# Lambda times alpha1 as one spread row, and a later place for the third batch's q loads, in a pooled-attention and residual-MLP kernel

## The chip, the cores and the metric

The kernel runs on one core of a Trainium2 chip, in one launch. The metric is the device time of one execution in microseconds (us), the median of several runs. In the profile PE is the matrix engine (PEld its weight loads), DVE, ACT and POOL are the vector, scalar and general engines, SP is the engine whose queue issues most transfers. PE, DVE, ACT, POOL and SP each work through their own instructions in order and wait for each other by semaphores.

## The reference

Eight batches, eight heads, 576 rows, head width 64. First attention with keys and values averaged over groups of 8 rows; then, on the heads side by side (x: 8 × 576 × 512), a residual block that mixes rows and then channels:

```python
k_p = k.reshape(B, H, Sp, 8, D).mean(axis=3);  v_p = ...          # Sp = 72
attn = softmax(scale * q @ k_p^T);  x = heads_side_by_side(attn @ v_p)
a1  = alpha1 * x + beta1
tok = einsum('ts,bsd->btd', w_tok, a1)
u   = x + lam * tok
a2  = alpha2 * u + beta2
out = u + lam * (maximum(a2 @ w_ch1, 0) @ w_ch2)                  # 512 -> 2048 -> 512
```

lam, alpha1, beta1, alpha2 and beta2 are vectors of 512.

## The kernel before, in words

The order of the work is written out by hand; there is no automatic scheduler. Batch 0's attention stands as a straight list of calls. From then on nine blocks of 512 rows (`n` from 0; four chunks of 128 rows each) go through the MLP, and beside block n the attention of batch n + 1 is placed. For each block a list `todo` of (due time, call) is filled and sorted; the due times only order the calls, and so the instructions of every engine. PSUM has six rotating buffers (`gp`) and two more (`psB`).

Attention of one head: `att_F` transposes q, `att_K` pools and transposes k, `att_S` or `att_S4` makes the scores and their exponentials (ET), `att_AV` multiplies by the pooled v and divides (reciprocal L562, product L564 into `x_tm`). `att_X` (L578) and `rest_X` (L571) multiply x by `lamal_bc`, lambda times alpha1 on all 128 partitions, and give `xs`, the operand of the row mix. `mix_T` (L614) multiplies w_tok by xs and adds x, giving u. ACT casts u to bf16 (L622), and for blocks after the first a transfer on SP's queue transposes it into `u_fm` (L633). `mlp_A` (L662) is the first MLP product; it takes a whole block's u_fm. `mlp_B` (L682) is the second.

The vectors lam, beta1 and alpha1 are loaded as rows into the tile `vecs` (row 0 of it is lam, row 2 alpha1). Before the change `spread_lam` multiplies a column of ones by lam's row in fp32 on PE (L304), which puts lam on all partitions, and ACT copies it to `lam_bc` (L305). `spread_al1` does that with one half of alpha1 (L311), and DVE multiplies it by lam_bc into a half of lamal_bc (L312). The first half is made before the first scores, the second between the scores of heads 6 and 7. lam_bc is also used by `scale_w2` (L721, sixteen pieces of w2 times lambda on DVE) and in block 0's output (L688). `bias_row` (L284) makes beta1 · lam, `more_constants` sets four constant regions that are needed only once w_tok is set up, and `keep_warm(n)` (L605) issues n matmuls on zeros whose result nobody reads.

At the start q, k and v come by transfers that POOL issues. The loads of batch 2 are issued during block 0: remainder rows (`load_rem`, L148), k (`load_k`, L93) and v (`load_v`, L160) from SP's queue, each behind a small DVE memset (the gate, due 15.3 to 15.4) that keeps them from starting earlier, and q (`load_q_bf`, L79) from POOL's queue, due 14.0 and 14.1. POOL does batch 1's att_X in three pieces (heads 2 and 3, 0 and 1, 4 and 5, due 13.8, 15.3 and 17.1), DVE the last (heads 6 and 7, due 18.8).

Of the kernel before, what the change touches and what calls it, by code (L numbers as in the profile page):

```python
# [11 lines left out]
ALU = mybir.AluOpType  # L12
# [11 lines left out]
def kernel(  # L24
# [18 lines left out]
    nc = tc.nc  # L43
# [8 lines left out]
    def gp(name):  # L52
        return psA.tile([P, 512], FP, tag="gp", name=name)
# [146 lines left out]
    lam_bc = const.tile([P, DM], FP, tag="lam_bc", name="lam_bc")  # L200
    lamal_bc = const.tile([P, DM], FP, tag="lamal_bc", name="lamal_bc")
# [3 lines left out]
    vecs = const.tile([65, 3, DM], FP, tag="vecs", name="vecs")  # L205
    ones_row = const.tile([1, P], FP, tag="ones_row", name="ones_row")
# [60 lines left out]
    for i in range(2):  # L267
# [11 lines left out]
                            in1=pool_v[0:32, 1:16:2], op=ALU.add)  # L279
    nc.vector.tensor_reduce(out=pool_rem, in_=pool_each, op=ALU.max, axis=AX.X)  # L280

    def bias_row(i):
        p0 = 64 - 64 * i
        nc.vector.tensor_tensor(out=xs_pool[i][p0:p0 + 1, 4, :], in0=vecs[p0:p0 + 1, 1],  # L284
                                in1=vecs[p0:p0 + 1, 0], op=ALU.mult)
# [5 lines left out]
    def more_constants():  # L291
        nc.vector.memset(ones_bf, 1.0)
        nc.vector.memset(ones_lo[0:64], 1.0)
        nc.vector.memset(ones_lo[64:128], 0.0)
        nc.vector.memset(wtT[:, :, S:640], 0.0)
# [2 lines left out]
        behind.memset(al2_bc[:, 0:1], 0.0)  # L298
        nc.sync.dma_start(out=al2_bc, in_=moe_alpha2.unsqueeze(0).to_broadcast((P, DM)))

    def spread_lam():

        ps = gp("ps_bc")
        nc.tensor.matmul(out=ps, lhsT=ones_row, rhs=vecs[0:1, 0])  # L304
        nc.scalar.copy(out=lam_bc, in_=ps)  # L305

    def spread_al1(half):

        ps = gp("ps_bc")[:, 0:256]
        cols = slice(256 * half, 256 * half + 256)  # L310
        nc.tensor.matmul(out=ps, lhsT=ones_row, rhs=vecs[0:1, 2, cols])  # L311
        nc.vector.tensor_tensor(out=lamal_bc[:, cols], in0=lam_bc[:, cols], in1=ps, op=ALU.mult)  # L312

    def setup_vectors():
        ps = gp("ps_vec")
# [115 lines left out]
    def double_k(u):  # L431

        nc.vector.tensor_copy(out=st1[0]["k"][u][:, :, 4], in_=st1[0]["k"][u][:, :, 0])
        if u == 0:
            cast_rem_k(nc.vector)
# [50 lines left out]
    def att_S(b, h):  # L486
        st = st1[b]
        u, r, hh = h // 4, h // 2 % 2, h % 2
        ET = ET_pool[u][:, h % 4]
        for half in range(2):  # L490
            n0, n = 256 * half, 256 + 64 * half
            ps_sc = gp("ps_sc")
            nc.tensor.matmul(out=ps_sc[0:SPG, 0:256], lhsT=kpT_pool[u][:, half, h % 4, :],  # L493
                             rhs=st["qT"][u][:, 2 * (h % 4):2 * (h % 4) + 2, :])
            if half:
                nc.tensor.matmul(out=ps_sc[0:SPG, 256:320], lhsT=kpT_pool[u][:, hh, h % 4, :],
                                 rhs=st["rem_qT"][:, :, h // 2::4].rearrange("p c i -> p i c"))
            nc.scalar.activation(out=ET[:, n0:n0 + n], in_=ps_sc[0:SPG, 0:n],
                                 func=AF.Exp, bias=0.0, scale=0.125)
        st["ET"][h] = ET  # L500
# [100 lines left out]
    def keep_warm(count):  # L601

        ps = psB.tile([P, DM], FP, tag="ch", bufs=2, name="ps_warm")
        for _ in range(count):
            nc.tensor.matmul(out=ps, lhsT=warm[:, 0:P], rhs=warm)  # L605
# [207 lines left out]
    att_F(0, 0)  # L813
    att_F(0, 1)
    cast_rem(0, nc.vector)
    more_constants()
    keep_warm(1)
    att_Frem(0, nc.scalar.copy)
    keep_warm(1)
    spread_lam()  # L820
    double_k(0)
    att_K(0, 0, None)
    spread_al1(0)
    bias_row(0)
    att_S(0, 0)
    att_S(0, 1)
    first_V(0, 0)
# [17 lines left out]
    att_S(0, 5)  # L845
    att_AV(0, 4)
    att_S(0, 6)
    spread_al1(1)
    att_AV(0, 5)
    att_X(0, 4, 6, nc.gpsimd, False)  # L850
    att_S(0, 7)
# [91 lines left out]
    for n in range(NBLK):  # L943
        todo = []
        for j in range(0 if n else 4, NJ):
            if n == 0 and j < 8:
                todo.append((j, lambda j=j: mlp_A(0, j, 0, 256)))
                todo.append((j + (1.01 if j < 7 else 0.3), lambda j=j: mlp_A(0, j, 256, 512)))
            else:
                at = 8 * (j // 4 % 2) + 4 * (j // 8) + j % 4 if n >= FIRST else j  # L950
                todo.append((at, lambda j=j: mlp_A(n, j)))
        for m in range(4 if n < FIRST else 0):
            for part in range(4):
                at = 16 + 2 * part + (m if m < 2 else 6 + m)
                todo.append((at, lambda m=m, part=part: mlp_B(n, m, part)))
        if n == 0:
            for i in range(3):
                for cc in range(4):
                    todo.append((17.0 + 2.0 * i + 0.5 * cc, lambda i=i, cc=cc: scale_w1(i, cc)))
            for piece, at in enumerate((13.9, 15.3, 19.2, 19.4, 24.5, 24.9, 25.3, 25.7, 26.9, 27.9)):  # L960
                todo.append((at, lambda k=piece: scale_w2(k // 4, k % 4)))
        if n == FIRST - 1:
            for piece, at in enumerate((0.5, 2.6, 5.2, 8.4, 10.9, 13.3)):
                todo.append((at, lambda k=piece + 10: scale_w2(k // 4, k % 4)))
            for s, i in enumerate((1, 3, 2)):
                for g in range(2):
                    todo.append((23.2 + 2.6 * s + 1.3 * g, lambda i=i, g=g: weight_sum(i, g)))
        if n == FIRST:
            for g in range(2):
                todo.append((1.2 + g, lambda g=g: weight_sum(4, g)))  # L970
        if n >= FIRST:
            last = n == NBLK - 1
            when = ((3, (4.6, 14.6)), (1, (8.6, 18.86)), (2, (8.8, 18.98)), (4, (22.3, 23.0)))
            if last:
                when = ((3, (4.6, 12.6)), (1, (8.6, 16.1)), (2, (8.8, 16.2)), (4, (18.6, 19.6)))
            for i, at in when:
                for g in range(2):
                    todo.append((at[g], lambda i=i, g=g: hidden_sum(n, i, g)))
            order = (1, 2, 6, 5, 7, 4, 3) if last else (1, 2, 4, 5, 6, 3, 7)
            for s, i in enumerate(order):  # L980
                for pp in range(2):
                    todo.append((16 + 2 * s + pp, lambda i=i, pp=pp: product(n, i, pp)))
                for part in range(2 if i == 7 else 1):
                    todo.append((17.05 + 2 * s + (1.9 if i == 1 and not last else 0) + 0.01 * part,
                                 lambda i=i, part=part: gather(n, i, part)))
            if last:
                for m in range(2):
                    todo.append((19.1, lambda m=m: store(n, m, 0, HALF)))
                    todo.append((25.2, lambda m=m: store(n, 2 + m, HALF, DM)))
                    todo.append((27.2, lambda m=m: store(  # L990
                        n, 2 + m, 0, HALF, (nc.sync, nc.scalar))))
                    todo.append((29.2, lambda m=m: store(
                        n, m, HALF, DM, ((nc.sync, nc.scalar)[m],) * 2)))
            else:
                for m in range(4):
                    todo.append((27.2 if m < 2 else 29.2, lambda m=m: store(n, m)))
        if n == 0:
            todo.append((6.2, lambda: setup_rowsum(4)))
            todo.append((8.3, setup_wtok_odd))
            for g in range(2, 4):  # L1000
                todo.append((4 * g - 0.8, lambda g=g: setup_bias(range(4 * g, 4 * g + 4))))
        b = n + 1
        if b < B:
            todo += attention(b)
            if b + 1 < B:
                new_batch(b + 1)
                gate = nc.vector if b == 1 else None
                for u in range(2):
                    at = (15.31 if b == 1 else 21.0) + 0.01 * u
                    todo.append((at, lambda b=b, u=u: load_k(b + 1, u, gate)))  # L1010
                    at = {1: 14.0, 2: 6.5}.get(b, 0.4) + 0.1 * u
                    todo.append((at, lambda b=b, u=u: load_q_bf(
                        b + 1, u, nc.vector if b == 2 else None)))
                    at = 15.35 + 0.01 * u if b == 1 else (6.7 if b == 2 else 3.5) + 4.0 * u
                    todo.append((at, lambda b=b, u=u: load_v(
                        b + 1, u, behind=nc.vector if b < 3 else None)))
                todo.append((15.3 if b == 1 else 20.9, lambda b=b: load_rem(b + 1, behind=gate)))
        for _, do in sorted(todo, key=lambda x: x[0]):
            do()
# [30 lines left out]
```

## Time and profile before

| | |
|---|---|
| time, median of 3 runs (lowest, highest) | 334.12 us (333.59, 334.47) |
| the profiled execution's own time, its span | 334.57 us, 332.9 us |
| PE / DVE / ACT / POOL busy, share of the span | 98% / 70% / 53% / 28% |
| costliest groups: L662, L785 (blocks from 2 on), L614 on PE | 133.7, 53.6 + 22.6, 44.9 us busy |
| second half of lamal_bc: L311 on PE, L312 on DVE | begin at 18.56 and 19.29 us |
| first matmul of the row mix, batch 0 and batch 1 | 22.81 and 55.48 us |
| first L662 of block 1 | 69.75 us |
| mean granted PE clock | 0.993 |

The span runs from the first instruction to the last; the time holds 1.67 us more around it. A busy PE in these profiles is not PE at its peak: the ends of matmuls are modelled, and neighbouring matmuls overlap, so where rates matter I go by the distance from one start to the next. In rows of a timeline the columns are start, length (both us), engine, line, operation, output<-input and shape; brackets hold the idle time before, and what ended it. The granted clock is a share of full speed.

### The profile page before, as it was taken

What the parts mean: (1) busy time and instruction counts of PE and PEld (TensorE: products, weight loads), DVE (VectorE), ACT (ScalarE), POOL (GpSimd) and SP (SyncE); (2) the same over time, 40 slices, a digit from 0 to 9 for tenths busy, and PEclk for the clock granted to TensorE, in tenths of its full rate; (3) what the DMA queues carried; (4) which work ended last, traced back from release to release, by engine and by line L of the source; (5) the groups of instructions that cost most, each with busy time, mean ns of one, the idle gap of its engine ahead of it and who ended that gap; (6) DMA issues with size and microseconds to landing.
All of it is one profiled execution on the core that took longest, in us unless ns stands there. A gap on an engine that the chain in (4) does not pass through costs nothing.

```text
span 332.9 us, 6509 instructions
## 1 busy us (share of the span) xinstructions
PE 325.5 (98%) x2531; PEld 209.2 (63%) x2531; DVE 234.5 (70%) x485; ACT 175.6 (53%) x322; POOL 94.8 (28%) x110
## 2 busy tenths in 40 slices
PE   6999999999999999999999999999999999999995
PEld 2667754455544567656775676558765866586584
DVE  6674189999769969677967797877778783263263
ACT  3584989448522871288128812682268325703710
POOL 8667828601237001900271027102510200000000
PEclk9799999999999999999999999999999999999999
DMA  8999979994994983399549943996340045003003
GB/s 117 198 210 270 271 159 206 208 227 87 146 246 105 211 159 121 72 223 181 152 89 219 182 136 73 187 189 194 61 140 2 0 61 145 2 0 127 1 32 97
DMA packets 66472, 45.81 MB, mean 138 GB/s; under 512 B 34397, under 2 KB 57061, under 8 KB 66442
## 3 DMA queue, kind: packets, MB, share of 16 engines
q1 hardware_dynamic: 52092, 32.67, 42.8%
q0 software_dynamic: 13824, 12.40, 22.8%
q8 instruction: 20, 0.33, 0.4%
q10 hardware_dynamic: 526, 0.34, 0.4%
q14 instruction: 10, 0.08, 0.1%
HBM read 38.30 MB, written 9.44 MB: 143 GB/s over the span
## 4 chain that ended last, share of the span: by engine, by line
PE 90%; DMA 5%; DVE 2%; POOL 1%; issue 0%; SPq 0%; ACTq 0%; ACT 0%; DVEq 0%; POOLq 0%
PE ps_h L662 36%; PE ps_w L785 26%; PE ps_tok L614 11%; PE ps_ch L682 7%; DMA rem_raw<-in_k_dram 3%; PE ps_s L513 2%; PE ps_av L556 2%; DMA rem_raw<-in_q_dram 2%; PE ps_kp L445 1%; PE ps_sc L493 1%; PE ps_r L520 1%; DVE x_tm L564 1%; PE ps_av L560 1%; DVE xs L578 0%; SPq L148 0%
## 5 line engine op out<-in xcount | busy, mean ns | idle before, releaser
L662 PE MATMUL ps_h<-u_fm,w 128*128 128x512 bf16 (+2 forms) x608 | 133.7, 369 | 0.2 <-DVE bias_cols L665 0.2
L669 ACT ACTIVATE H<-ps_h,bias_cols 128x512 bf16<-128x512 f32 x144 | 98.2, 688 | 56.4 <-PE ps_h L662 55.4
L662 PEld LDWEIGHTS <-w 128*128 128x128 bf16 x608 | 65.5, 114 | 49.8 <-issue 2.4
L785 PEld LDWEIGHTS <-H 128*128 128x128 bf16 x560 | 53.5, 98 | 10.8 <-DVE u_sb L803 1.2
L622 ACT CAST u_bf<-u_sb 128x512 bf16<-128x512 f32 x32 | 19.8, 618 | 70.9 <-issue 39.9
L785 PE MATMUL ps_w<-w_l,H 128*128 128x256 bf16 x448 | 53.6, 273 | 0.0
L803 DVE TENSOR_TENSOR u_sb<-u_sb,ps_w 128x512 f32<-128x512 f32 x54 | 36.3, 682 | 17.1 <-PE ps_w L785 17.1
L578 POOL TENSOR_TENSOR xs<-x_tm,lamal_bc 128x512 bf16<-128x512 f32 x12 | 15.5, 1297 | 108.8 <-DVE x_tm L564 108.7
L614 PE MATMUL ps_tok<-xs,wtT 128*128 128x512 bf16 (+3 forms) x200 | 44.9, 380 | 0.5 <-DVE xs L578 0.5
L618 DVE TENSOR_TENSOR u_sb<-x_tm,ps_tok 128x512 f32<-128x512 f32 (+1 forms) x40 | 27.3, 682 | 10.0 <-PE ps_tok L614 9.9
L564 DVE TENSOR_TENSOR x_tm<-ps_av,rec 128x320 f32<-128x320 f32 x64 | 31.4, 491 | 2.7
L542 ACT ACTIVATE ET<-ps_s 72x512 f16<-72x512 f32 x56 | 32.3, 591 | 0.0
L614 PEld LDWEIGHTS <-wtT 128*128 128x128 bf16 (+3 forms) x200 | 17.3, 100 | 16.8 <-issue 1.1
L562 DVE RECIPROCAL rec<-ps_av 128x5 f32<-128x5 f32 x64 | 12.1, 190 | 17.0 <-PE ps_av L560 16.7
L483 DVE TENSOR_TENSOR v_u<-v_u 72x1024 f32<-72x1024 f32 (+1 forms) x24 | 22.7, 948 | 0.2
L785 PE MATMUL ps_w<-w_t,h_s 128*128 128x256 bf16 x168 | 22.6, 272 | 0.0
L682 PEld LDWEIGHTS <-H 128*128 128x128 bf16 x128 | 11.9, 98 | 13.7 <-issue 0.4
L754 DVE TENSOR_TENSOR H<-H,H 128x1024 bf16<-128x1024 bf16 x14 | 9.7, 690 | 14.3 <-ACT H L669 14.2
L785 PEld LDWEIGHTS <-h_s 128*128 128x128 bf16 x168 | 16.4, 98 | 4.1
L187 POOL TENSOR_TENSOR k_bf<-k_raw 128x512 bf16<-128x512 f32 x14 | 18.4, 1317 | 1.1
L754 DVE TENSOR_TENSOR h_s<-H 128x1024 bf16<-128x1024 bf16 x21 | 14.4, 686 | 6.0 <-ACT H L669 5.8
L185 POOL TENSOR_TENSOR k_raw<-k_raw 128x512 f32<-128x512 f32 x14 | 18.4, 1316 | 0.6 <-DMA k_raw<-in_k_dram 0.6
(148 smaller groups left out, 369.0 us busy)
## 6 DMA issues: line engine op xcount, KB each, us to landing
out_dram<-u_sb SPq DMA_DIRECT2D x29, 256.0 KB
k_raw<-in_k_dram SPq DMA_DIRECT2D x12, 512.0 KB
v_u<-in_v_dram SPq DMA_DIRECT2D x12, 512.0 KB
q_bf<-in_q_dram POOLq DMA_DIRECT2D x16, 256.0 KB, 7.0
w<-in_moe_w_ch_dram POOLq DMA_DIRECT2D x6, 512.0 KB, 12.0
out_dram<-u_sb SPq DMA_DIRECT2D x11, 128.0 KB
w<-in_moe_w_ch_dram POOLq DMA_DIRECT2D x1, 1024.0 KB, 14.3
k_raw<-in_k_dram POOLq DMA_DIRECT2D x2, 512.0 KB, 16.7
```

The costliest lines, as they stand in the source:

```text
L483: nc.vector.tensor_tensor(out=out, in0=t[:, :, 0:width], in1=t[:, :, width:2 * width], op=ALU.add)
L542: nc.scalar.activation(out=o, in_=i, func=AF.Exp, bias=0.0, scale=0.125)
L564: nc.vector.tensor_tensor(out=x[:, 1 - odd:6 - odd, dd:dd + D], in0=av[:, :, 0:64], in1=rec.unsqueeze(2).to_broadcast((P, 5, D)), op=ALU.mult)
L614: nc.tensor.matmul(out=ps_tok[p0:p1], lhsT=wtT[0:kk, at, P * c:P * c + p1 - p0], rhs=xs_pool[i][0:kk, sc, :], start=(sc == 0), stop=(sc == 4))
L618: nc.vector.tensor_tensor(out=s["u"][p0:p1, :], in0=x[p0:p1, 1 + c if c < 4 else 5 - 5 * i, :], in1=ps_tok[p0:p1, 0:DM], op=ALU.add)
L622: nc.scalar.copy(out=s["u_bf"], in_=s["u"])
L662: nc.tensor.matmul(out=ps_h[:, t0:t1 + one], lhsT=w1_of(cc, j), rhs=rhs, start=(cc == 0), stop=(cc == 3))
L669: nc.scalar.activation(out=H4[n, j // 4][:, j % 4, :], in_=ps_h, func=AF.Relu, bias=bias_cols[:, j:j + 1], scale=1.0)
L682: nc.tensor.matmul(out=ps, lhsT=H_of(n, j)[:, 128 * m:128 * m + 128], rhs=(w2l if n else w2)[j // 4][:, j % 4, :], start=(j == 0), stop=(j ...
L754: nc.vector.tensor_tensor(out=o, in0=a, in1=b, op=op)
L785: nc.tensor.matmul(out=ps, lhsT=stat(j), rhs=moving(j), stop=(j == 7), start=(first and (pp == 0 or alone) and j == 0), skip_group_check=True)
L803: nc.vector.tensor_tensor(out=o, in0=o, in1=banks[key, "both"], op=ALU.add)
```

## The change

lambda · alpha1 is now formed as a row of 512 on one partition (`lamal_row`, DVE, in place of alpha1 in vecs), and one product of 512 columns spreads it; DVE copies it to lamal_bc. lam_bc is spread by a second product of 512 columns, at the place where the second half of alpha1 was spread, and DVE, no longer ACT, copies it. Two more warm-up matmuls stand where spread_lam stood. more_constants moves behind the first scores' preparation. In block 0, two of the pieces of scale_w2 get later due times (the order of DVE changes by one piece: the second, which stood ahead of the gate memsets, now follows batch 1's att_X). Batch 2's q loads get the due time 17.12, which puts them on POOL behind all of batch 1's att_X. SP's order stays as it was.

```diff
-    def spread_lam():
+    def lamal_row():
+        nc.vector.tensor_tensor(out=vecs[0:1, 2], in0=vecs[0:1, 2], in1=vecs[0:1, 0], op=ALU.mult)
+
+    def spread(i, out):
         ps = gp("ps_bc")
-        nc.tensor.matmul(out=ps, lhsT=ones_row, rhs=vecs[0:1, 0])
-        nc.scalar.copy(out=lam_bc, in_=ps)
-
-    def spread_al1(half):
-        ps = gp("ps_bc")[:, 0:256]
-        cols = slice(256 * half, 256 * half + 256)
-        nc.tensor.matmul(out=ps, lhsT=ones_row, rhs=vecs[0:1, 2, cols])
-        nc.vector.tensor_tensor(out=lamal_bc[:, cols], in0=lam_bc[:, cols], in1=ps, op=ALU.mult)
+        nc.tensor.matmul(out=ps, lhsT=ones_row, rhs=vecs[0:1, i])
+        nc.vector.tensor_copy(out=out, in_=ps)
...
     cast_rem(0, nc.vector)
-    more_constants()
+    lamal_row()
     keep_warm(1)
     att_Frem(0, nc.scalar.copy)
-    keep_warm(1)
-    spread_lam()
+    keep_warm(3)
     double_k(0)
     att_K(0, 0, None)
-    spread_al1(0)
+    spread(2, lamal_bc)
     bias_row(0)
+    more_constants()
     att_S(0, 0)
...
     att_S(0, 6)
-    spread_al1(1)
+    spread(0, lam_bc)
     att_AV(0, 5)
...
-            for piece, at in enumerate((13.9, 15.3, 19.2, 19.4, 24.5, 24.9, 25.3, 25.7, 26.9, 27.9)):
+            for piece, at in enumerate((14.2, 19.2, 19.4, 20.3, 24.5, 24.9, 25.3, 25.7, 26.9, 27.9)):
                 todo.append((at, lambda k=piece: scale_w2(k // 4, k % 4)))
...
-                    at = {1: 14.0, 2: 6.5}.get(b, 0.4) + 0.1 * u
+                    at = {1: 17.12, 2: 6.5}.get(b, 0.4) + (0.01 if b == 1 else 0.1) * u
                     todo.append((at, lambda b=b, u=u: load_q_bf(
                         b + 1, u, nc.vector if b == 2 else None)))
```

## The prediction

> **What bounds the kernel now.** I read the page first, then the busy time by stretches, then each engine's timeline around the edits. The page:
>
> ```profile
> span 332.9 us, 6509 instructions
> ...
> PE 325.5 (98%) x2531; PEld 209.2 (63%) x2531; DVE 234.5 (70%) x485; ACT 175.6 (53%) x322; POOL 94.8 (28%) x110
> ```
>
> PE is idle for 7.4 us of 332.9: 1.4 before its first matmul, 0.9 waiting for the first q, 3.7 behind its last matmul, and little else. So an edit pays only where PE stands still, runs at half clock, or carries filler. The stretches (us; then length and PE, PEld, DVE, ACT, POOL busy; granted clock, DMA share, GB/s) show two such places:
>
> ```profile
> 10.00:11.00 1.00, 0.88 (x4) 0.35 (x5) 0.54 (x2) 0.54 (x2) 0.93 (x3) 1.00 1.45 196
> 11.00:12.00 1.00, 1.00 (x7) 0.89 (x8) 0.97 (x2) 0.80 (x3) 0.75 (x2) 0.52 1.45 196
> 12.00:14.00 2.00, 2.00 (x13) 1.01 (x12) 0.67 (x3) 0.75 (x4) 0.76 (x1) 0.50 1.40 217
> 14.00:16.00 2.00, 2.00 (x50) 1.97 (x49) 1.60 (x6) 1.63 (x6) 0.35 (x1) 0.89 1.05 211
> ...
> 50.00:52.00 2.00, 2.00 (x21) 1.04 (x20) 1.71 (x11) 2.00 (x4) 1.94 (x4) 1.00 0.12 19
> 52.00:54.00 2.00, 2.00 (x20) 1.05 (x19) 1.87 (x6) 2.00 (x3) 1.84 (x3) 1.00 1.19 171
> 54.00:56.00 2.00, 1.51 (x8) 0.55 (x7) 1.94 (x3) 2.00 (x3) 1.66 (x2) 1.00 1.33 262
> 56.00:60.00 4.00, 4.00 (x20) 1.79 (x19) 3.96 (x7) 3.75 (x8) 3.48 (x4) 1.00 1.10 321
> ```
>
> The clock is half for 3.4 us from about 11.0 (0.48 + 0.50·2 + 0.11·2 = 1.7 us lost). DMA is idle until 52 and full from there to 69. The PE timeline of the second place, with the POOL, DVE and SP rows that lead to it:
>
> ```profile
> 52.24 2.76 PE L682 MATMUL ps_ch<-w,H 128*128 128x512 bf16 x12
> 55.48 1.25 PE L614 MATMUL ps_tok<-xs,wtT 128*128 128x512 bf16 x5 [0.49 <-DVE xs L578]
> ...
> 64.56 5.35 PE L682 MATMUL ps_ch<-w,H 128*128 128x512 bf16 x24
> 69.75 1.03 PE L662 MATMUL ps_h<-u_fm,w 128*128 128x512 bf16 x4
> ```
> ```profile
> 50.10 1.57 POOL L79 DMA_DIRECT2D q_bf<-in_q_dram  x2
> 51.74 1.26 POOL L578 TENSOR_TENSOR xs<-x_tm,lamal_bc 128x512 bf16<-128x512 f32 x1
> ```
> ```profile
> 49.88 0.84 DVE L721 TENSOR_TENSOR w_l<-w,lam_bc 128x512 bf16<-128x512 bf16 x1
> 50.67 0.06 DVE L145 MEMSET rem_raw<- 128x4 f32 x1
> ...
> 53.81 1.62 DVE L578 TENSOR_TENSOR xs<-x_tm,lamal_bc 128x512 bf16<-128x512 f32 x1
> ```
> ```profile
> 50.76 1.25 SPq L148 DMA_DIRECT2D rem_raw<-in_q_dram  x2
> ...
> 53.48 1.00 SPq L93 DMA_DIRECT2D k_raw<-in_k_dram  x2
> 54.73 2.45 SPq L160 DMA_DIRECT2D v_u<-in_v_dram  x4
> ...
> 61.86 5.01 SPq L633 DMA_TRANSPOSE u_fm<-u_bf  x3
> ```
>
> The reader is to see a hole before 55.48, and that block 1 begins (L662, 69.75) as soon as L682 is done (64.56 + 24 × 0.216 = 69.74). Block 1 needs all four transposes of u_fm; the trace's record of landings has the last at 69.52. So this queue is only 0.2 us ahead of PE: k_raw, v_u, two stores and the transposes go through one SP queue in order.
>
> **Start (to 18 us).** ACT loses L305 (0.59 us at 9.34). Its next copy, kpT at 10.00, waited for K's matmuls (last begun at 9.79), so 0. DVE gains `lamal_row`: nearest row, bias_row L284 with one partition of 512, 0.68 us. It waits for alpha1, which lands at 8.17 in the record, so it runs 8.25 to 8.93. Behind it in DVE's queue are double_k and the two casts of rem_k, and behind those K's fourth matmul and L451. double_k, begun at 8.43, begins at 8.9. PE's three warm-up matmuls end at 8.5; it issues three K matmuls, waits to 9.15, runs the other 13 at 29 ns and L451 to 9.65, 0.15 earlier than now. The product of 512 then takes 1.05 us (L304: 8.18 to 9.23) where the half took 0.62, so the first score matmul goes from 10.52 to about 10.82, but the second waits for DVE's kpT and stays at 10.93 (now 10.94). Sum 0; if alpha1 lands later, all of that lateness is lost. On DVE the copy of lamal_bc (0.42 to 0.69, L477 and L618; I take 0.69), bias_row 0.68 and the four memsets (7.67 to 8.44, 0.77) run 10.95 to 13.05, under the cover of the score and v matmuls at half clock: the vp cast begins at 13.35. Margin 0.3, cost 0. The rotating PSUM buffers lose one user: 0.
>
> **The clock.** It halves at 11.04, after a stretch (7.6 to 11.0) in which PE was almost never idle. But 1.66 us of that were fp32 products of one row (L304, L311); the bf16 columns are about 28% of it. In the preceding 3.4 us bf16 work filled about 59% and the clock held. The change makes it about 41% (two more warm-ups, 0.43 us), between the two, so a coin toss. If the clock holds, PE has v done by 12.2, but the cast now waits for DVE's memsets to 13.05; head 0's product comes 0.38 earlier, the second K 14.72 − 0.70 = 14.02. So it is worth 0 or −0.7. I take 0, the clock seen.
>
> [...]
>
> **Lambda's spread at 18.6 us.** 1.05 for 0.63 on PE (L311: 18.56 to 19.19), +0.42, in a stretch where PE has no gap. DVE copies 0.69 instead of L312's 0.42, begun 0.42 later: done at 20.40, not 19.71. Heads 5, 6, 7 follow at 0.66 each, so the xs piece L578 begins at 22.6 instead of 21.91 and the first mix matmul (22.81) at 23.45: +0.64. At 36.53 PE waits 0.25 for batch 1's k sum, which hangs on rem_raw's landing (33.27) behind alpha2's broadcast, and that does not move. So +0.39 is left.
>
> **Batch 1's mix, 50 to 55 us.** scale_w2 (0.84) leaves DVE at 49.88, where the next wait is on PE's products: the last x piece ends at about 53.6 instead of 53.8. The q issues (1.57) leave POOL, whose pieces then run 50.2, 52.0 to 53.3, with rest_X to 53.8. DVE's L578 no longer shares its time with POOL's and takes 0.75 as at 21.91, not 1.62: done at 54.4, before PE is free (52.24 + 12 × 0.216 = 54.83). The hole of 0.65 closes; bounds −0.65 and, if L578 stays slow, −0.2. DVE pays scale_w2 back after 54.7, then idles 0.74 at 62.6: 0.
>
> **The loads behind it.** The gate memsets come 0.7 earlier, so rem_raw is issued at 50.05 and k_raw at 52.8. The four rem_raw issues at 0.65 each do not fill the engines, which q did before. k_raw's packets start at about 54.5 instead of 55.75: −1.25. q is now issued at 53.85 to 55.4 and its packets fall into k_raw and v_u. Its 1024 packets went at 388 per us, 2.6 us of all engines; v_u and q side by side at 82 to 83 us kept only that joint rate (49 of 100 and 179 of 388 per us, sum 0.95). So everything behind in the SP queue is 2.6 − 1.25 = 1.35 later, and u_fm's last transpose lands at about 70.9 rather than 69.52. Block 1 starts at about 71.0 rather than 69.75: +1.25, and the closed hole only makes PE wait longer. Bounds: −0.65 (no delay; PE comes at 69.1) and +2.4 (the early gate brings nothing). I take +1.25, since the engines are full from 52 to 69.
>
> **Sum** for the likeliest case: 0 + 0 + 0.39 + 1.25 = +1.64. The profiled execution took 334.57 (span 332.9 and 1.67 around it): 336.2. It stood 0.45 above the median 334.12, so the median becomes 335.7.
>
> **Rivals.** (1) As the forecast, but the clock holds at 11 us: 0.7 less at the start, which also uses up the 0.25: 0.39 becomes about −0.06, sum +1.2, 335.3. For it: more full-array columns; against: 41% may be too little. (2) The queue is not late: this decides if u_fm's last transpose lands before 69.1 + shift, because the earlier gate and idle engines absorb q. Then −0.65 counts: 333.9 with the clock dropped, 333.4 with it held; the kernel is faster. For it: DMA was idle until 52; against: it is full afterwards, with 0.2 us to spare. (3) PE's new wait of some 2 us halves the clock again at 71: 3.4 us at half is up to +1.7, 337.4. For it: 11 us shows that such a drop follows a thin stretch; against: dense bf16 still fills over 40% of any such window. (4) The product as a row does nothing to the end, since PE is bound later: that is inside (2).
>
> **Chances.** Forecast 0.40, rival 1 0.26, rival 2 0.24, rival 3 0.10. The range reaches from 333.4 to 336.8, leaving out rival 3 and part of rival 2; the unknown sizes (±0.5 on the queue) are in it. About 0.3% (1.0 us) is what a measurement can tell from no change. Below 333.12: part of rival 2, 0.10; above 335.12: the forecast, two thirds of rival 1 and rival 3, 0.63; the rest 0.27. Faster and slower cases do not balance: the likeliest one's own range is 335.1 to 336.3.
>
> **What would show it.** In the changed profile: L614 follows L682 with no hole near 55; a new PE wait of 1.5 to 2 us on the u_fm transposes before the first L662 of block 1, near 71; q_bf packets between 55 and 60; first mix matmul near 23.4 (clock half at 11) or 22.7 (clock full). I am wrong if block 1 starts without a wait, or if the start is more than 1 us off.

## The result, and the profile after

The changed kernel takes 335.6 us (median of 6 executions, 334.81 to 336.9); before has 333.4 over six executions (334.12 was the median of the first three of them). The ratio is 1.0069 (95% interval 1.004 to 1.0097): about 2.3 us slower, where the prediction had 1.6 and a time of 335.7. Ratios leave out executions more than 1.5% above the fastest of their kernel (one in experiment 1, six in experiment 3). The profiled execution took 336.59, with 334.8 of span and 1.79 around it.

Lines of after are 4 lower than those of before: L578 is now L574, L614 is L610, L633 is L629, L662 is L658, L682 is L678; the products are L307, the row L302, the v cast L473 (before L477). First a line of the page, then PE's longest wait (total, times, longest, us):

```profile
PE 325.9 (97%) x2531; PEld 209.3 (63%) x2531; DVE 234.5 (70%) x486; ACT 174.8 (52%) x321; POOL 95.5 (29%) x110
```
```profile
PE ps_h L658 <- DMA u_fm<-u_bf: 1.7, 1, 1.7
```

PE has the same 2531 matmuls and nearly the same busy time as before (325.5), but it stands still 1.5 us longer, and the new waits have names: one on the u_fm transposes, two in batch 0's K (0.8 each, in brackets further down). The first is seen best in PE's timeline, with the POOL, DVE and SP rows that lead to it (the row of L578 is one of before):

```profile
52.99 2.75 PE L678 MATMUL ps_ch<-w,H 128*128 128x512 bf16 x12
55.58 1.24 PE L610 MATMUL ps_tok<-xs,wtT 128*128 128x512 bf16 x5
...
64.65 5.35 PE L678 MATMUL ps_ch<-w,H 128*128 128x512 bf16 x24
71.69 1.03 PE L658 MATMUL ps_h<-u_fm,w 128*128 128x512 bf16 x4 [1.68 <-DMA u_fm<-u_bf]
```
```profile
52.88 1.27 POOL L574 TENSOR_TENSOR xs<-x_tm,lamal_bc 128x512 bf16<-128x512 f32 x1
...
54.63 1.57 POOL L79 DMA_DIRECT2D q_bf<-in_q_dram  x2
```
```profile
53.61 1.27 POOL L578 TENSOR_TENSOR xs<-x_tm,lamal_bc 128x512 bf16<-128x512 f32 x1
```
```profile
54.42 0.81 DVE L574 TENSOR_TENSOR xs<-x_tm,lamal_bc 128x512 bf16<-128x512 f32 x1
```
```profile
53.87 1.06 SPq L93 DMA_DIRECT2D k_raw<-in_k_dram  x2
55.18 2.56 SPq L160 DMA_DIRECT2D v_u<-in_v_dram  x4
...
62.22 6.60 SPq L629 DMA_TRANSPOSE u_fm<-u_bf  x3
```

The hole before the first L610 is gone: it follows L678 at once. Without the issue of q among its pieces POOL is done with the last one at 54.15, and DVE's L574 behind it takes 0.81; in before POOL's last piece (53.61 to 54.88) ran beside DVE's, which took 1.62. But the q loads are issued at 54.63 instead of 50.10, beside k_raw and v_u, and the four transposes behind those in SP's queue have their last landing at 71.55 (before 69.52). In the records of the single packets q moves from 58.50 to 68.32. Beside it the 2 KB packets of v_u and of the two stores behind it take from 59.29 to 69.33, where before has 58.56 to 67.40; k_raw's come a little earlier (55.08 to 59.03, before 55.69 to 59.37). PE, done at 70.0, waits 1.68 for the transposes. From the last L678 group ahead of the mix to block 1, before needs 69.75 − 52.24 = 17.51 us, after 71.69 − 52.99 = 18.70: the 1.19 us lost here are a gain of half a microsecond at the hole and 1.7 of new wait. The other 0.75 us (52.99 for 52.24) are older, from the start:

```profile
8.69 0.26 PE L441 MATMUL ps_kp<-pool_main,k 128*128 128x64 bf16 x3 [0.78 <-DMA k<-in_k_dram]
9.79 0.55 PE L441 MATMUL ps_kp<-pool_main,k 128*128 128x64 bf16 x13 [0.84 <-DVE k L429]
...
11.41 0.41 PE L489 MATMUL ps_sc<-qT,kpT 128*72 128x256 bf16 x2
```
```profile
8.91 0.68 DVE L302 TENSOR_TENSOR vecs<-vecs 1x512 f32<-1x512 f32 x1 [2.00 <-DMA vecs<-in_moe_alpha_dram]
```

The row product waits for alpha1, which in this execution landed at 8.82, not at 8.17 as before; the doubling of k queues behind it on DVE, and K behind that. The first three K products wait for batch 0's k itself, which landed at 8.64; before's first K product stood behind the spread of lambda until 9.23. The stretches (start:end; length, then PE, PEld, DVE, ACT, POOL busy; granted clock, DMA share, GB/s):

```profile
11.00:12.00 1.00, 1.00 (x7) 0.56 (x6) 0.83 (x2) 0.25 (x1) 0.88 (x2) 0.90 1.42 187
12.00:14.00 2.00, 2.00 (x11) 1.12 (x10) 1.69 (x7) 1.05 (x4) 0.76 (x1) 0.50 1.36 221
...
54.00:56.00 2.00, 2.00 (x11) 0.88 (x9) 1.90 (x4) 2.00 (x3) 1.92 (x4) 1.00 0.46 102
56.00:60.00 4.00, 4.00 (x20) 1.86 (x19) 3.96 (x7) 4.00 (x8) 3.88 (x5) 1.00 1.19 315
```

The clock is halved for 3.4 us here too (from 11.80 instead of 11.04). And the DMA share is 0.46 from 54 to 56, where it was 1.33 before: the q packets have left a time in which the engines had little to do and lie in the full stretch behind 56 (a share of 1.19 to 1.35 from 56 to 68).

**How times are compared below.** In part of the executions of every kernel but one the PE clock is halved near the start (their mean granted clock is below 0.997; in the profiles that show it, the clock falls to 0.50 between 11.04 and 21.7 us), and those take longer (by the medians 1.2 to 3.3 us, and 5.5 for one kernel). So beside the ratio over all executions I give their number and the median of the others (at least 0.997). For before, measured anew with each of four groups of runs, these are 14 halved of 35, 5 of 35, 3 of 18 and 6 of 17 (28 of 105), and medians of 333.43, 333.12, 333.25 and 333.30; for after 2 of 6, and 335.44, so at full clock the loss is 2.0.

### The profile page after: what moved, and what is told of

Read it like the earlier page. It is cut to its first block, busy times and chain, and to the rows that moved or that the text cites. A ratio compares the mean times of both kernels' runs of the same rounds, so it can differ in the third digit from the quotient of the medians.

```text
span 334.8 us, 6509 instructions
## 1 busy us (share of the span) xinstructions
PE 325.9 (97%) x2531; PEld 209.3 (63%) x2531; DVE 234.5 (70%) x486; ACT 174.8 (52%) x321; POOL 95.5 (29%) x110
## 4 chain that ended last, share of the span: by engine, by line
PE 92%; DMA 3%; DVE 1%; SPq 1%; ACTq 1%; issue 0%; POOL 0%; ACT 0%; DVEq 0%
PE ps_h L658 38%; PE ps_w L781 26%; PE ps_tok L610 11%; PE ps_ch L678 6%; PE ps_av L552 3%; PE ps_s L509 2%; DMA vecs<-in_moe_alpha_dram 2%; DMA u_fm<-u_bf 1%; SPq L629 1%; PE ps_kp L441 1%; PE ps_sc L489 1%; PE ps_r L516 1%; PE ps_bc L307 1%; DVE u_sb L614 1%; PE ps_av L556 1%; PE ps_v L468 0%
## 5 line engine op out<-in xcount | busy, mean ns | idle before, releaser
L658 PE MATMUL ps_h<-u_fm,w 128*128 128x512 bf16 (+2 forms) x608 | 133.7, 369 | 1.9 <-DMA u_fm<-u_bf 1.7
L658 PEld LDWEIGHTS <-w 128*128 128x128 bf16 x608 | 65.4, 114 | 51.8 <-issue 4.3
L574 POOL TENSOR_TENSOR xs<-x_tm,lamal_bc 128x512 bf16<-128x512 f32 x12 | 15.5, 1299 | 111.4 <-DVE x_tm L560 111.2
L610 PE MATMUL ps_tok<-xs,wtT 128*128 128x512 bf16 (+3 forms) x200 | 44.9, 380 | 0.0
L614 DVE TENSOR_TENSOR u_sb<-x_tm,ps_tok 128x512 f32<-128x512 f32 (+1 forms) x40 | 27.3, 683 | 9.6 <-PE ps_tok L610 9.5
L610 PEld LDWEIGHTS <-wtT 128*128 128x128 bf16 (+3 forms) x200 | 17.4, 100 | 16.0 <-issue 1.1
L678 PEld LDWEIGHTS <-H 128*128 128x128 bf16 x128 | 11.9, 98 | 13.7 <-issue 0.4
```

What stands on the lines that cost most here:

```text
L610: nc.tensor.matmul(out=ps_tok[p0:p1], lhsT=wtT[0:kk, at, P * c:P * c + p1 - p0], rhs=xs_pool[i][0:kk, sc, :], start=(sc == 0), stop=(sc == 4))
L614: nc.vector.tensor_tensor(out=s["u"][p0:p1, :], in0=x[p0:p1, 1 + c if c < 4 else 5 - 5 * i, :], in1=ps_tok[p0:p1, 0:DM], op=ALU.add)
L658: nc.tensor.matmul(out=ps_h[:, t0:t1 + one], lhsT=w1_of(cc, j), rhs=rhs, start=(cc == 0), stop=(cc == 3))
L678: nc.tensor.matmul(out=ps, lhsT=H_of(n, j)[:, 128 * m:128 * m + 128], rhs=(w2l if n else w2)[j // 4][:, j % 4, :], start=(j == 0), stop=(j ...
```

## Experiments

**1. The two parts, each alone.** After with the q loads back at their old due time:

```diff
-                    at = {1: 17.12, 2: 6.5}.get(b, 0.4) + (0.01 if b == 1 else 0.1) * u
+                    at = {1: 14.0, 2: 6.5}.get(b, 0.4) + 0.1 * u
```

> The changed kernel with batch 2's q loads back at due time 14.0 and 14.1. Theory A (the q loads now stand in the DMA engines between batch 2's rem_raw and v, so block 1's u_fm transposes land 2.0 us late and PE waits 1.7 us at 71): the wait goes, u_fm lands near 70 and block 1 begins near 70.4; the hole at 55 us opens again to about 0.5 us; time 1.2 to 1.6 us under the changed kernel, about 334.1. Theory B (the loss is at the start: the row product waits for alpha1 and lambda's spread is twice as wide): no gain, 0 to 0.5 us slower than the changed kernel, since only the hole comes back.

Before with the q loads at the new due time (the same line, the other way round):

> The kernel before with one edit: batch 2's q loads at due time 17.12 and 17.13. The gate memsets stay near 50.7 us, as in the changed kernel. Theory A: the hole at 55 closes, but u_fm's last transpose lands near 71.5 and block 1 begins near 71.6 after a wait of 2 us or more; 1.5 to 2.0 us slower than before, nearly the whole loss of the change. Theory B: 0 to 0.6 us faster than before.

After with the old due times of q and of the w2 pieces, so only the new start is left:

```diff
-            for piece, at in enumerate((14.2, 19.2, 19.4, 20.3, 24.5, 24.9, 25.3, 25.7, 26.9, 27.9)):
+            for piece, at in enumerate((13.9, 15.3, 19.2, 19.4, 24.5, 24.9, 25.3, 25.7, 26.9, 27.9)):
```

> The changed kernel with both edits to block 0's list undone (q loads at 14.0, scale_w2 at its old due times): only the row product, the two wide spreads, the warm-ups and the moved constants are left. Theory A: everything from 37 us on is 0.4 to 0.8 us later than before, the hole at 55 stays, no wait at 70; 0.4 to 0.8 us slower than before. Theory B: the whole loss, 1.5 to 2.2 us slower than before.

Before with the new times of the w2 pieces alone:

> The kernel before with scale_w2's new due times alone. Both theories: the gate memsets and rem_raw's issue come 0.75 us earlier, DVE's last x piece 0.15 us earlier, still beside POOL's and so still slow; the hole at 55 shrinks by 0.1 to 0.2 us. Theory A: 0 to 0.3 us faster than before, within noise.

| kernel | ratio to before | halved | median of the others, against before's | last L678/L682 group to block 1 |
|---|---|---|---|---|
| after, q back | 1.0028 (0.9997 to 1.006) | 5 of 12 | 333.97, +0.54 | 17.55 |
| before, q late | 1.0043 (1.0012 to 1.0074) | 5 of 12 | 334.70, +1.27 | 18.93 |
| new start only | 1.0029 (0.9998 to 1.006) | 6 of 12 | 334.02, +0.59 | 17.54 |
| before, w2 times | 0.9985 (0.9955 to 1.0015) | 2 of 12 | 333.23, −0.20 | 17.52 |
| after | 1.0069 (1.004 to 1.0097) | 2 of 6 | 335.44, +2.0 | 18.70 |

The two parts nearly add up: +1.27 for the place of the q loads (1.5 to 2.0 had been expected) and +0.59 for the start, +2.0 together. The w2 times cost nothing that can be measured. The PE timeline of before with q late has the whole effect of the q part by itself:

```profile
69.50 4.48 PE L662 MATMUL ps_h<-u_fm,w 128*128 128x512 bf16 x20 [1.91 <-DVE u_sb L689]
```

The wait is put down to a DVE step that had long been done; the last u_fm transpose landed at 69.36, so it is the transfer again. PE was done with L682 at 67.6.

**2. The q loads early instead of late.** If the loss is q's packets in a full stretch, q should cost nothing where the engines stand almost still (a DMA share of 0.17 from 48 to 50 and 0.12 from 50 to 52 in before). After with one number changed:

```diff
-                    at = {1: 17.12, 2: 6.5}.get(b, 0.4) + (0.01 if b == 1 else 0.1) * u
+                    at = {1: 12.0, 2: 6.5}.get(b, 0.4) + 0.1 * u
```

> The changed kernel with one number altered: the third batch's two q loads are due at 12.0 instead of 17.12, so POOL issues them before all of its adds of batch 1's attention, when it idles (40 to 48 us), and the packets should move near 50 to 53 us, while the DMA engines stand almost still. Theory A (the loss is q's packets lying between rem's and v's in the DMA engines and pushing the u_fm transposes back): TensorE then has neither the hole at 55 nor the 1.7 us wait ahead of block 1; the transposes land near 69.3 or before, and the time is about 2.0 us under the changed kernel, 333.5, ratio to before about 1.000. Theory B (the SP queue is late for another reason, the gate memsets or the added weight pieces, whatever q does): the wait ahead of block 1 stays above 1 us and the time stays near 335.5. Theory C (q cannot move earlier, because its buffer comes free only late): POOL's queue stalls behind the issue and the mix of batch 1 is late, 336 or more.

The ratio is 1.0041 (1.001 to 1.0072), with 6 of 12 halved, four of them at a mean clock of 0.985 to 0.989, as low as the profiled one with its two half windows. So the expected ratio of 1.000 did not come. The six others have a median of 333.13, against 333.12 of before and 335.44 of after. This profile fell on an execution that was halved twice, so it begins late, and the stretch is what counts:

```profile
41.03 1.51 POOL L79 DMA_DIRECT2D q_bf<-in_q_dram  x2
```
```profile
56.77 1.24 PE L610 MATMUL ps_tok<-xs,wtT 128*128 128x512 bf16 x5
...
65.83 5.35 PE L678 MATMUL ps_ch<-w,H 128*128 128x512 bf16 x24
71.18 1.03 PE L658 MATMUL ps_h<-u_fm,w 128*128 128x512 bf16 x4
```

No hole ahead of the first L610 (54.17 + 12 × 0.216 = 56.76), no bracket ahead of L658: 17.01 us for the stretch, 1.69 less than after. POOL issues q at 41 us, when it has nothing else to do. That settles the q part: the SP queue was late because of q's place and not because of the gates or the w2 pieces, which are as in after here.

The same in before, with the new w2 times:

> The kernel before, with its own start, the changed kernel's four times of the weight pieces, and the q loads due at 12.0. Theory A (q out of POOL's pieces closes the hole of 0.5 to 0.65 us at 55, and q out of the way of v and the transposes keeps block 1 on time): no hole, block 1 as soon as TensorE is done with the mix, 0.5 to 0.65 us under before, ratio 0.998. Theory B (closing the hole only lengthens the wait for u_fm): ratio 1.000. Theory C (the q buffer is not free so early): slower, ratio 1.003 or more.

Ratio 0.9994 (0.9968 to 1.002), 5 of 12 halved; the others 332.40 against 333.12, −0.72, a little more than the hole (0.5 to 0.65), as theory A has it. The stretch is 16.85, without a wait. The ratio, with the halved executions in it, does not show this. The new start costs 333.13 − 332.40 = 0.73 by this pair, 0.59 by the first group.

**3. What in the start costs.** The start alone, with the row product behind the doubling of k:

```diff
-    lamal_row()
     keep_warm(1)
...
     double_k(0)
+    lamal_row()
```

> The start of the changed kernel alone (the q loads and the weight pieces as before), with one step moved: the product of lambda and alpha1 stands behind the doubling of k instead of ahead of it in VectorE's queue. In the run with the new start alone TensorE waited 1.2 us for VectorE's doubled k in K. Theory A (the new start's cost is that the row holds K back until alpha1 has landed): the wait falls to about 0.6, the first K matmuls come 0.5 to 0.7 earlier, and the kernel ends at 0.4 to 0.6 us less than the new start alone, ratio to before about 1.001. Theory B (the cost is the 512-wide product, which ends later in any order, and the constants ahead of the v cast): the row then delays the product itself, the first score matmul stays where it is, and the ratio stays at 1.003.

Of 12 executions 10 were halved, six of them at a mean clock of 0.978 to 0.979 like the profiled one, which was at half clock for four windows in a row (12.90 to 26.55). The ratio over the other six is 1.0067 (1.0033 to 1.01). The two that kept the clock took 333.80 and 333.91, +0.74: no gain, as far as two executions can tell. It speaks too against alpha1's landing as the main cost that in the profile with q early the row ran at 7.76, alpha1 having landed at 7.66, and that this kernel's start still costs the 0.73 above. The four profiles of the new start that have full clock until about 13 us show another wait of PE, 0.70 to 0.73, on the v cast (here the run with the new start only, DVE and PE):

```profile
13.30 0.22 DVE L295 MEMSET wtT<- 128x192 uint32 x1
13.44 0.36 DVE L473 CAST vp<-ps_v 72x256 f16<-72x256 f32 x1
```
```profile
13.85 0.29 PE L552 MATMUL ps_av<-vp,ET 72*128 72x66 f16 x4 [0.70 <-DVE vp L473]
```

The constants (L292 to L295) stand right ahead of the cast. From the second score matmul to this L552 are 13.85 − 11.49 = 2.36 us; with the old start at full clock 12.61 − 10.85 = 1.76, or 1.75 in two other profiles. At half clock both have 2.6 (13.83 − 11.22 before, 14.31 − 11.73 after), because PE is then later than DVE. To test it: after with q early, and the constants back in their old place.

```diff
     cast_rem(0, nc.vector)
+    more_constants()
     lamal_row()
...
     bias_row(0)
-    more_constants()
```

> The changed kernel with the q loads at 12.0 and one call moved back to its old place: the four constant memsets (more_constants, 0.77 us of VectorE) stand ahead of the row product again, where VectorE waits for alpha1, and no longer between the bias row and the cast of v. Theory A (of the new start's cost, 0.6 us are the wait of TensorE for the v cast that queues behind the memsets whenever the clock is not halved): the wait of 0.7 near 13 us is gone, from the second score matmul to the first product with v are 1.75 us instead of 2.36, and the executions that keep their clock have a median 0.4 to 0.6 under the same kernel with the memsets late, about 0.5 under those of before. Theory B (the cost is the late product of 512 columns and alpha1's landing alone): the wait goes but comes back at the next k, and the median of those executions stays where before's is.

The wait is gone and the distance is 12.72 − 10.97 = 1.75. But in this execution the row ran at 8.15 behind the constants and PE waited 0.6 for the doubled k. The time says little: ratio 0.999 (0.9965 to 1.0015), 5 of 12 halved, the others 333.12 against 333.30 of before, −0.18, where the same kernel with late constants stood at +0.01. That is 0.2 of the 0.4 to 0.6 expected, and not more than the medians scatter: the wait is shown, its price in the total is not.

The other half of the start is the product of 512 between the heads. In before with q early and the new w2 times, lambda stays where it was spread, and one product of the row takes the place of both halves (the row is formed behind the doubling of k):

```diff
+    def spread_lamal():
+        ps = gp("ps_bc")
+        nc.tensor.matmul(out=ps, lhsT=ones_row, rhs=vecs[0:1, 2])
+        nc.vector.tensor_copy(out=lamal_bc, in_=ps)
...
-    spread_al1(0)
+    spread_lamal()
...
-    spread_al1(1)
```

> The run above with one more step: the two half products of alpha1 become one product of a row of 512 (lambda times alpha1) right after the first K, with lambda itself spread early by ScalarE as before, so no product stands between the heads at 18.6 us; the row's multiplication stands behind the doubling of k. Theory A (a product of one row between the heads costs its length, 0.63 us, and at the start there is room for it): 0.6 us less than the run above, ratio 0.996. Theory B (the start has no room: the longer product at 10 us pushes the first scores by 0.4 and the wait at 36.5 us takes the rest): no less than the run above, ratio 0.998.

From the first product with v to the first mix matmul are 8.7 to 8.9 us in three profiles of the old start at full clock, 9.14 in two of the new, and 20.50 − 12.49 = 8.01 here. So the late product adds 0.25 to 0.4 to this distance, and without it the distance is 0.7 to 0.9 shorter than in before. Again the times do not show it: 332.37 against 332.40 of the run without this step, each in 7 executions, so the 0.6 expected by theory A did not come. Ratio 0.9998 (0.9973 to 1.0023), 5 of 12 halved.

**4. What stands ahead of a halving.** The changes of the clock record lie whole multiples of 3.41 us apart: 6.83, 3.41 and 317.44 us in the profile of before, 6.83, 3.41 and 320.85 in that of after. In the first ten profiles I cut the first 40 us into windows of that length, and summed in each the time of the matmuls (0.21 us per 512 columns, where those of L682 start 0.216 apart; 1.05 in fp32, L304 from 8.18 to 9.23), weighted by the rows of 128 that the record gives for them. Seven full-clock windows were followed by a half-clock one, at shares of 0.22 to 0.37 of the window; of the 87 that were not, the lowest lie at 0.37, 0.38 and 0.40. Without the weight the two kinds overlap (0.53 to 0.74 against 0.55 and more). That is a pattern of these profiles; what decides the clock, they do not show. If the pattern holds further, the clock should be kept beside the same product with 128 rows, 127 of them zero. In the last kernel, with two memsets on DVE before 5 us, where it has time:

```diff
+    nc.vector.memset(ones_all, 1.0)
...
+    nc.vector.memset(lamal_bc, 0.0)
...
-        nc.vector.tensor_tensor(out=vecs[0:1, 2], in0=vecs[0:1, 2], in1=vecs[0:1, 0], op=ALU.mult)
+        nc.vector.tensor_tensor(out=lamal_bc[0:1], in0=vecs[0:1, 2], in1=vecs[0:1, 0], op=ALU.mult)
...
-        nc.tensor.matmul(out=ps, lhsT=ones_row, rhs=vecs[0:1, 2])
+        nc.tensor.matmul(out=ps, lhsT=ones_all, rhs=lamal_bc)
```

> The previous run with both edits (q loads at 12.0, lambda spread early, one product of 512) with one thing altered: the product that spreads lambda times alpha1 has 128 rows instead of one, of which 127 are zero, so it computes the same, and should take the same 1.1 us. It tells what halves the clock. In ten profiles a 3.4 us window is followed by a half-clock window where the streaming time of its matmuls, each weighted by its rows over 128, is below about 0.38 of the window (seven of seven), and kept at full clock where it is above. Theory A (that share decides): with 128 rows the product adds 0.3 to every window around it, so no early window falls below 0.38; none of 12 runs is halved early where 5 of 12 were, and the median falls from 333.2 to 332.3, ratio to before about 0.997. Theory B (the halving follows idle time, whatever the rows): 4 to 6 of 12 runs are halved and the median stays at 333.2. Theory C (a product of 128 fp32 rows takes longer than of one): the first scores are later and the time grows by that.

The median falls from 333.20 to 332.14, ratio 0.9973 (0.9949 to 0.9997): the fastest kernel of the study, and its whole interval lies below before. Not all of that is the clock, though: the executions that kept it have 331.98, 1.27 under those of before in their group, where the kernel without the tall product was 0.75 under. The profiles do not say where that half microsecond comes from. 2 of 12 executions were halved, not the 0 expected, for one window each by their mean clock. The row has become an array-high product of the same length:

```profile
9.37 1.12 PE L312 MATMUL ps_bc<-vecs,ones_row 1*128 1x512 f32 x2
```
```profile
9.39 1.10 PE L314 MATMUL ps_bc<-lamal_bc,ones_all 128*128 128x512 f32 x2
```

The first line is the kernel without, the second with; 1*128 and 128*128 are rows and columns of the array. The same in after, for its first product only:

> The changed kernel with only its first product (lambda times alpha1) made 128 rows high, 127 of them zero; the late spread of lambda stays one row. Theory A (the share of rows decides the clock): the halving near 11 to 13 us disappears; one that begins near 19 to 20 us, behind the late product, can remain in about a third of the runs. At most 4 of 12 runs are halved, and the median falls from 335.6 to 335.1 or a little less, ratio 1.005. Theory B (idle time decides): 5 or 6 of 12 are halved, near 12 us as before, and the median stays at 335.6, ratio 1.007. In both the wait on the u_fm transposes ahead of block 1 (1.7 us) stays.

None of 7 executions was halved, early or late, and the median is 335.1 (ratio 1.0049, 1.003 to 1.0067), with the 1.7 us wait on u_fm as it was. Over all runs, kernels with the old start were halved in 40 of 141 executions, those with the new one in 24 of 54 (without the moved row's 10 of 12), those with the tall product in 2 of 19. These counts do not settle it: the two kernels with the tall product were measured in the group in which before, with its old start, was halved in only 3 of 18, and the two without it in other groups. The profiles say more. The three later ones fit, with one more halving behind a window of 0.36, and none elsewhere. Together these are 125 full-clock windows, 8 of them with a halving behind them, all at 0.37 or less, and none of the others lies lower than 0.37. And one window tests the weighting: from 7.74 to 11.16 in the kernel with the tall product the share is 0.62, it would be 0.31 had the product one row, and the clock was kept.

## Why the prediction was right, and where it was not

**The number** is right to 0.1 us, partly by luck: the loss is 2.3 and not 1.6, and before's own median, taken from three executions, stood 0.7 too high.

**The loads behind block 0's mix: right in mechanism and size.** The forecast was 1.25 us through a new wait of 1.5 to 2 us near 71. Measured: a wait of 1.68 that ends at 71.69, 1.19 more for the stretch, 1.27 in the executions at full clock. Two sub-steps were off. The early gate was to bring k_raw 0.7 forward; it was issued at 53.87, 0.39 later than before, which is 0.36 earlier against the start's shift of 0.75. Its first packet still came as forecast: at 55.08 for 55.69, so 1.36 earlier against that shift, where 1.25 was expected. And q's packets were to move between 55 and 60, into k_raw and v_u; they moved from 58.50 to 68.32, and it was v_u and the stores that they slowed. The late q issue (53.85 forecast, 54.63 seen) is the forecast one plus that shift. Rival 2, that idle engines absorb q, fell for the due time 17.12 but holds for 12.0: DMA does have the room, before 52: its share from 48 to 50 is 0.17 in before and 1.34 in before with q early and the new w2 times.

**The hole at 55: right.** Zero after, and −0.72 where it closes without the wait behind it.

**Lambda's spread late: right** in the profiles, near enough: from the first product with v to the first mix matmul +0.25 to +0.43 at full clock, and +0.53 in the profiled pair (0.42 forecast on PE). In that pair the first mix matmul is at 23.82, 1.01 later than before (23.45 was forecast), and K at 37 us (37.55 for 36.78) only 0.77 later: before waits 0.25 ahead of it and after does not, the give-back that the prediction counted on. In the profiles at full clock neither start has that wait.

**The start: the sum of 0 failed.** It was worked out at half clock, where DVE's four memsets are hidden ("Margin 0.3, cost 0"). The profiled execution of before had that cover, but 101 of 141 executions with the old start keep the clock; there the v cast comes late, and PE loses 0.6. The paragraph on the clock did see that wait, but as a smaller gain from a held clock, against a profile that was the rarer case. Second, the row waits for alpha1, which in the profile of after landed 0.65 later, so the first score matmul is at 11.41 and not 10.82; the condition was named ("all of that lateness is lost"), its chance was not. Together the start costs 0.6 to 0.7 at full clock, where 0.39 was forecast. The distances in the profiles sum to more (0.6 and up to 0.4, and up to 1.2 in K), and the executions do not show each of them: where the rest is given back at full clock stays open.

**The clock: the toss came out the other way.** The two extra warm-ups were to fill the window to 41%. The new start was halved in 44% of the executions, the old in 28%; in each of the three groups that have both, the new one was halved more often, but by little in the first (11 of 24 against 21 of 59) and the last (5 of 12 against 6 of 17). In the profile of after the window of 8.39 to 11.80 holds 22%, with the waits for k and alpha1 in it, and behind the late product the clock fell in three of the profiles with the new start, at 18.8 to 21.7 us. Where the windows lie varies from run to run: the changes are 3.41 us or a multiple of it apart, the first one is at 4.2 to 6.7 us, and the same kernel is halved in some executions only. PE did not stand idle ahead of a halving: it was busy in 66% to 97% of each such window, the few-row products counted as busy.

**Rival 3**, a second drop behind the new wait at 71, did not come: the granted clock is 1.00 from 15.21 us to the end of the span. (In the chances, 0.63 for a time above 335.12 is a slip: its parts, 0.40, 0.17 and 0.10, are 0.67.)

## What to carry to other kernels

A load that is moved out of an engine's way has to be followed to the DMA engines: moved later it met two other queues in a full stretch and cost 1.3 us, moved earlier, where the issuing engine was idle and the stretch ahead had room, it cost nothing that could be measured and closed the same hole. Before a step is costed at nothing, ask whether the cover is there in every execution: here it was a half-clock window that two of seven have. And where executions differ by 2 us through the clock, compare those that kept it.

## What the runs showed of the hardware that was not expected

- In these profiles the PE clock was halved behind eight windows with a row-weighted share of 0.22 to 0.37, while PE was busy in 66% to 97% of each: in that sum a one-row fp32 product of 1.05 us counts 0.01 us. A 128-row product took the same time (1.10 against 1.12 us), and the one window whose share hung on it (0.62, not 0.31) kept the clock. This is a pattern with one direct test and not a proof: the weighting was chosen after the fact, on ten profiles, the counts of halved executions differ as much between groups of runs (14 of 35 and 5 of 35 for before) as between kernels, and the two halvings left with the tall product are not explained.
- A halving can last: the profile of the moved row has four half windows on end (13.65 us); six executions of that kernel have its mean clock and took some 5.8 us more than the two that kept it.
- The landing of a 2 KB row varies between executions by more than the steps that were planned around it: alpha1 landed at 8.17 and 8.82 in the pair of profiles, and from 7.50 to 8.82 over all thirteen.
